# One block of linear attention and a routed expert on one core: q in plain column order, M in seven passes, reciprocals fetched per chunk, weights loaded earlier

## The chip, the core and the metric

The kernel runs on one core of a Trainium2 chip. The core has TensorE (PE, matrix products; PEld is its weight load), VectorE (DVE), ScalarE (ACT), GpSimd (POOL) and SyncE (SP, which here only issues DMAs), and 16 DMA engines that move data between the chip's memory (DRAM) and the on-chip SBUF. TensorE writes to PSUM, eight banks of 2 KB a partition. The metric is the device time of one execution, in microseconds (us).

## The reference

x has 2048 tokens of D = 640 numbers. Two things are added to it.

```python
xn  = layernorm(x)                                  # per token
q, k, v = split(xn @ wqkv)                          # 32 heads of 20 columns
phi(t) = where(t > 0, t + 1, exp(t)) + 1e-6
kv  = einsum("shd,she->hde", phi(k), v)             # 20 x 20 per head
z   = sum over tokens of phi(k)
o   = (phi(q) @ kv) / (phi(q) . z + 1e-6)           # per head
A   = o @ wo

r   = x_B @ w_r                                      # routing score of each token
idx = the 8 tokens with the largest r
y   = (silu(xs @ w_gate) * (xs @ w_up)) @ w_down     # xs: those 8 tokens of xn
B   = xn, with y * sigmoid(r[idx]) added at rows idx

out = x + A + B
```

In the whole program the second part gets xn as its input, so that its residual is xn and the scores are xn @ w_r.

## The kernel before

The tokens are cut into 16 tiles of 128 (T), the 640 columns into 5 chunks of 128 (KC). All of the program is one function. The schedule is manual: each engine executes its instructions in the order in which the code issues them, and semaphores that follow from tiles and buffers let an engine wait for another. So an instruction that waits holds everything behind it on the same engine, and a DMA that waits holds the DMAs behind it on the queue of its issuer. A DMA also waits until an earlier one that used the same one of eight semaphores has landed.

**Start (to L399).** ln_half and ln_aggr take a tile's statistics (VectorE), and a power on GpSimd makes the standard deviation; ln_norm makes xn (L191). TensorE transposes xn of tiles 0 to 2 itself (tr_tile, L200), from tile 3 on a DMA does it (L196). k_mm (L236) and q_mm (L248) are the products with wk and wq. k_mm(0) runs five matmuls of 512 columns and then five of 129 (128 and the column of the scores); behind them come the transposes of tile 1 and their evictions (L206).

**The loop (L401).** Slot t does k_mm(t), ga_mm(t - 1) and q_mm(t) on TensorE; meanwhile VectorE does the statistics of a later tile, the normalisation of a tile with its transpose, and the last steps of phi for q of t - 1 and k of t (L225); ScalarE does the exp and relu halves (L213, L216). Statistics run three tiles ahead and normalisation two. In slot 5 (CATCH) both do one tile more, and from then on are four and three ahead. ga_mm sums xn^T phi(k), from which kv follows as wv^T (xn^T phi(k)). late_loads issues one load a slot on SP: x's last two quarters in slots 2 and 5, w_gate from slot 6, w_up from 9, wv and wo in 12 to 15; w_down follows behind the loop. From slot 12 residual adds xn to x in place (L360) and keep writes the sums to xcp in DRAM (L363); the last four tiles come behind the search for the top eight.

**Behind the loop.** The scores are transposed, the eight largest are found on VectorE, and GpSimd copies their columns of xnT into xsT (L537). Meanwhile TensorE sums the rest of xn^T phi(k): gb1 (L489) columns 384 to 640 of xn, gb2 (L590) the last 128 columns of phi(k). z_mm (L460) sums phi(k) over tokens; zpart goes from rows to partitions by small DMAs (zrel). pden (L571) has the 32 denominators of all tokens: a group of 32 partitions for each block of 512 tokens; ScalarE takes the reciprocal as exp(-ln). Two tiles of gb2 come next, then gate and up (gu, L606), then the rest of gb2.

**q's columns.** q_mm takes every fifth column of wq as one block of weights, `wq[:, kc, m::KC]`, so that partition p of chunk m holds column 5p + m, which belongs to head p // 4 in every chunk. So one tile rb of reciprocals serves all five chunks. It is made by a write of rden to DRAM that repeats each row four times (rscr, L621) and two loads (L625). norm(j) multiplies a block of 512 tokens in place (L632).

**M and the output.** kv is kept block diagonal, masked, in kvT (L670). M (L728) is kv times wo, in q's column order: for each chunk m, 8 blocks of 80 rows of wo make two chained passes of four column groups of 32. M's copies (L737) go to ScalarE for chunks 0, 1 and 3 and VectorE for 2 and 4. y (L688) is made before, copied, and added by GpSimd's indirect DMA to the eight rows of xcp (L697); behind that scatter SP loads xcp back into x_sb (L702). The output of tile t is five chunks of pqT times M (L743); VectorE adds x_sb while reading PSUM (L751), and ACT's and SP's queues write the result in turn (L762). Four PSUM buffers rotate, so tile t + 4 waits for the addition of tile t.

Of the kernel before, what the change touches and what calls it, by code (L numbers as in the profile page):

```python
# [11 lines left out]
H = 32  # L12
# [13 lines left out]
PAD = 16  # L26
# [5 lines left out]
CATCH = 5  # L32
# [12 lines left out]
def kernel(  # L45
# [47 lines left out]
    kvT = sb([EB, PAD + NEB * KC * 2 * PAD], BF16, "kvT")  # L93
# [4 lines left out]
    rscr = dram.tile([NTB * P, TBLK], BF16, name="rscr")  # L98
# [32 lines left out]
    headg = sb([P, NTB, H], BF16, "headg")  # L131
    nc.vector.memset(headg[:], 1.0)
    mask80 = sb([EB, KC, 4, 4], BF16, "mask80")
# [21 lines left out]
    head_select(headg[:], [(0, NTB), (-4, H)], 1, 4)  # L155
# [73 lines left out]
    def k_mm(t, tag="A"):  # L229
# [5 lines left out]
        for kc, (a, b) in order:  # L235
            nc.tensor.matmul(  # L236
                ps[:, a:b],
                lhsT=xnT[:, kc, t * P : (t + 1) * P],
                rhs=wk[:, kc, a:b],
                start=(kc == 0), stop=(kc == KC - 1),  # L240
            )
        return ps

    def q_mm(t, tag="B"):
        ps = pair(tag, f"q{t}")
        for m in range(KC):
            for kc in range(KC):
                nc.tensor.matmul(  # L248
                    ps[:, m * P : (m + 1) * P],
                    lhsT=wq[:, kc, m::KC],  # L250
# [43 lines left out]
    ln_aggr(2)  # L294
# [8 lines left out]
    def small_consts(t):  # L303
# [18 lines left out]
        elif t == 6:  # L322
            head_select(mask80[:], [(0, KC), (-DH, 4), (0, 4)], 1, DH)
# [17 lines left out]
    def late_loads(t):  # L341
        def part(dst, src, a, b):
            nc.sync.dma_start(dst[:, a:b, :], src[:, a:b, :])

        wv_v = wqkv_v[:, :, 2 * D : 3 * D]
        plan = {
            2: (x_sb, x_v, 8, 12), 5: (x_sb, x_v, 12, 16),
            6: (wg, kcF, 0, 2), 7: (wg, kcF, 2, 4), 8: (wg, kcF, 4, 5),
            9: (wu, kcU, 0, 2), 10: (wu, kcU, 2, 4), 11: (wu, kcU, 4, 5),
            12: (wv, wv_v, 0, 2), 13: (wv, wv_v, 2, KC), 14: (wo, wo_v, 0, 4), 15: (wo, wo_v, 4, 8),  # L350
            16: (wd, kcD, 0, 6), 17: (wd, kcD, 6, 12),
        }
        if t in plan:
            part(*plan[t])

# [21 lines left out]
    kp = k_mm(0, "A")  # L377
    tr1a, tr1b = bank("D1", "tr1a").bitcast(BF16), pair("C", "tr1b").bitcast(BF16)
    tr_tile(1, tr1a, 0, 2)
    tr_evict(1, tr1a, 0, 2, nc.scalar.copy)  # L380
    tr_tile(1, tr1b, 2, KC)
    tr_evict(1, tr1b, 2, KC, nc.vector.tensor_copy)
# [18 lines left out]
    for t in range(2, T):  # L401
# [11 lines left out]
        if t > 12:  # L413
            residual(4 * (t - 13) + 3)
        phi_vec(pk[:, t, :], ker, False)
        qer = phi_act(qp, "q")
        if 11 < t < T - 1:
            for u in range(4 * (t - 12), 4 * (t - 12) + 3):
# [3 lines left out]
        if t > 12:  # L422
            keep(4 * (t - 13), 4 * (t - 12))
# [48 lines left out]
    zpart = sb([P, D], F32, "zpart", tag="rb")  # L472
    nc.scalar.copy(zpart[:], zp[:, 0:D])
# [6 lines left out]
    late_loads(T)  # L480
    late_loads(T + 1)
# [54 lines left out]
    for c in range(C):  # L536
# [7 lines left out]
        out=zm[:], in0=headg[:, 0, :].unsqueeze(1).to_broadcast([P, KC, H]),  # L544
# [17 lines left out]
    for t in range(T - 4, T):  # L562
        residual(t)
    keep(T - 4, T)
# [33 lines left out]
    for t in range(2):  # L598
        gb2(t)


    gu = pair("A", "gu")
    for a, w in enumerate((wg, wu)):
# [9 lines left out]
    sg = sb([P, FJ], F32, "sg")  # L613
# [5 lines left out]
    rb = sb([P, S], BF16, "rb")  # L619

    nc.sync.dma_start(  # L621
        rscr[:].rearrange("(p r) n -> p r n", r=4), rden[:].unsqueeze(1).to_broadcast([P, 4, TBLK])
    )
    for j in (0, 2):
        nc.sync.dma_start(  # L625
            rb[:, j * TBLK : (j + 2) * TBLK].rearrange("p (j n) -> p j n", j=2),
            rscr[j * P : (j + 2) * P, :].rearrange("(j p) n -> p j n", j=2),
        )

    def norm(j):  # L630
        sl = pqT[:, :, j * TBLK : (j + 1) * TBLK]
        nc.vector.tensor_tensor(  # L632
            out=sl, in0=sl,
            in1=rb[:, j * TBLK : (j + 1) * TBLK].unsqueeze(1).to_broadcast([P, KC, TBLK]),
            op=ALU.mult,
        )

    for t in range(2, 12):
# [14 lines left out]
    pkv = (bank("D0", "pkv0"), bank("D1", "pkv1"), pair("B", "pkv2"))  # L653
    groups = ((0, 2, 4), (1, 3, 5), (6, 7))

    def kv_mm(i):
        for n, b in enumerate(groups[i]):
# [8 lines left out]

    def kv_evict(i):
        n, w = len(groups[i]), KC * 2 * PAD
        lo, step = groups[i][0], groups[i][1] - groups[i][0]
        nc.vector.tensor_tensor(  # L670
            out=kvT[:, PAD : PAD + NEB * w].rearrange("e (b m c) -> e b m c", b=NEB, m=KC)[
                :, lo : groups[i][-1] + 1 : step, :, 0:PAD
            ],
            in0=pkv[i][0:EB, 0 : n * EB].rearrange("e (b c m) -> e b m c", b=n, m=KC),
            in1=mask80[:].rearrange("e m h j -> e m (h j)").unsqueeze(1).to_broadcast([EB, n, KC, PAD]),
            op=ALU.mult,
        )

    for i in range(3):
        kv_mm(i)  # L680
        kv_evict(i)
    norm(0)
# [39 lines left out]
    for m in range(KC):  # L722
        pm = Acc("CBADC"[m], f"M{m}")
        for a, b in halves:
            for i in range(2):
                for g in range(4):
                    o = PAD + ((2 * g + i) * KC + m) * 2 * PAD - i * PAD
                    nc.tensor.matmul(  # L728
                        pm.at(a, b)[32 * g : 32 * g + 32, :],
# [77 lines left out]
```

## Time and profile before

| What | us |
|---|---|
| three runs | 112.4, 111.48, 112.14 (median 112.14) |
| the profiled execution, whole | 111.62 |
| its span from the first to the last instruction | 109.9 |
| TensorE busy | 105.5 |
| VectorE busy | 86.1 |
| ScalarE busy | 55.1 |
| GpSimd busy | 37.9 |
| moved by DMA | 23.09 MB, mean 210 GB/s |

Stretches in the span: start to 8.84 us, the loop with its first slots to 62.48, the sums and the search to 79.81, kv and y to 82.28, M to 85.00, the output to 107.0, the last writes to 109.9.

In timelines the columns are: start, duration, engine (a q behind it is the engine's sequencer, which issues DMAs), line, operation, output and inputs, count, and in brackets the idle time before it with what ended it. In rows by line: busy time with the mean of one in ns, and idle time before it. In the rows of DMA issues: size of one and the median time from issue to landing.

### The profile page before, as it was taken

The page shows a single profiled execution, that of the slowest core. Times are in us where ns is not written, and L with a number is a line of the kernel's source. Part 1 is how long each engine was busy: PE and PEld are TensorE (multiplying, and loading weights), DVE is VectorE, ACT ScalarE, POOL GpSimd, SP SyncE. Part 2 cuts the span into 40 slices and gives each one's busy share as a digit, 9 for nine tenths or more (in the row PEclk, how much of TensorE's full clock was granted, in tenths as well). Part 3 has the DMA queues.
Part 4 walks back from the last instruction along what each step waited for, and adds up shares of the span by engine and source line. Part 5 has one row for each costly group of instructions (what it writes and reads, how often), then busy time and mean ns, then how long its engine had stood idle before and what let it go on. Part 6 is the DMA issues. An engine that isn't in the chain of part 4 may idle for free.

```text
span 109.9 us, 2999 instructions
## 1 busy us (share of the span) xinstructions
PE 105.5 (96%) x1183; PEld 69.3 (63%) x1183; DVE 86.1 (78%) x205; ACT 55.1 (50%) x102; POOL 37.9 (34%) x83
## 2 busy tenths in 40 slices
PE   6998999999999999999999999999999999999990
PEld 2456866777577766777667744447995555555560
DVE  6889999887999889875999896951348967698680
ACT  4037987778867797777977745068028000000000
POOL 5414195989889955770000000240008100000000
DMA  2998164930569999998859970899541289997333
GB/s 72 335 375 292 33 36 75 283 66 3 118 177 321 220 267 280 316 305 224 290 187 285 292 257 5 232 378 372 175 145 51 15 228 323 340 387 277 128 119 119
DMA packets 25358, 23.09 MB, mean 210 GB/s; under 512 B 10624, under 2 KB 24064, under 8 KB 25344
## 3 DMA queue, kind: packets, MB, share of 16 engines
q1 hardware_dynamic: 22784, 20.43, 66.5%
q10 hardware_dynamic: 2384, 2.43, 6.4%
q8 instruction: 9, 0.15, 0.6%
q0 software_dynamic: 176, 0.04, 0.6%
q14 instruction: 5, 0.04, 0.1%
HBM read 14.94 MB, written 5.81 MB: 189 GB/s over the span
## 4 chain that ended last, share of the span: by engine, by line
PE 76%; DVE 10%; POOL 8%; issue 3%; DVEq 0%; POOLq 0%
PE o L743 14%; PE k L236 13%; PE q L248 13%; PE gbA L489 6%; PE gaC L259 5%; PE warm L271 4%; PE gbC L590 4%; POOL sq L176 3%; DVE st L163 2%; PE gaD L259 2%; DVE pk L225 2%; PE M L728 2%; POOL sc L178 2%; DVE xn L191 2%; PE gu L606 2%
## 5 line engine op out<-in xcount | busy, mean ns | idle before, releaser
L248 PEld LDWEIGHTS <-wq 128*128 128x128 bf16 x400 | 24.2, 117 | 3.4
L236 PE MATMUL k<-wk,xnT 128*128 128x512 bf16 (+1 forms) x160 | 24.8, 301 | 0.3 <-ACT xnT L206 0.3
L248 PE MATMUL q<-xnT,wq 128*128 128x128 bf16 x400 | 24.9, 220 | 0.0
L743 PEld LDWEIGHTS <-pqT 128*128 128x128 bf16 x165 | 12.8, 98 | 9.3
L236 PEld LDWEIGHTS <-xnT 128*128 128x128 bf16 x160 | 12.3, 98 | 8.5 <-ACT xnT L206 0.9
L213 ACT ACTIVATE eq<-q 128x640 bf16<-128x640 f32 x16 | 11.2, 703 | 10.5 <-PE q L248 10.5
L225 DVE SCALAR_TENSOR_TENSOR pk<-ek,rk 128x640 bf16<-128x640 bf16 x16 | 13.2, 824 | 3.6 <-ACT rk L216 3.4
L743 PE MATMUL o<-M,pqT 128*128 128x512 bf16 x110 | 15.8, 300 | 0.0
L176 POOL TENSOR_TENSOR sq<-sq,half 128x1 bf16<-128x1 bf16 x16 | 12.5, 778 | 6.2 <-DVE sc L175 4.0
L163 DVE BATCH_NORM_STATS2 st<-x_sb 128x6 f32<-128x320 bf16 x32 | 14.1, 480 | 0.4 <-DMA x_sb<-in_A_x_dram 0.4
L225 DVE SCALAR_TENSOR_TENSOR pqT<-eq,rq 128x640 bf16<-128x640 bf16 x16 | 13.2, 823 | 0.7 <-ACT rq L216 0.7
L213 ACT ACTIVATE ek<-k 128x640 bf16<-128x640 f32 x16 | 11.3, 705 | 1.6 <-PE k L236 0.4
L751 DVE TENSOR_TENSOR o_t<-o,x_sb 128x640 bf16<-128x640 f32 x11 | 8.8, 820 | 3.3 <-DMA x_sb<-xcp 1.7
L216 ACT ACTIVATE rq<-q 128x640 bf16<-128x640 f32 x16 | 11.2, 700 | 0.0
L216 ACT ACTIVATE rk<-k 128x640 bf16<-128x640 f32 x16 | 11.2, 699 | 0.0
L259 PE MATMUL gaC<-pk,xn 128*128 128x512 bf16 x32 | 9.5, 378 | 0.2 <-DVE pk L225 0.2
L537 POOL COPY xsT<-xnT 128x5 bf16 x8 | 1.9, 312 | 21.7 <-DVE icol L551 21.7
L178 POOL TENSOR_TENSOR sc<-sq,neg 128x1 f32<-128x1 bf16 x12 | 8.6, 716 | 0.9
L191 DVE TENSOR_SCALAR xn<-x_sb,sc 128x640 bf16<-128x640 bf16 (+2 forms) x17 | 6.9, 412 | 1.2 <-POOL sc L179 1.0
L489 PE MATMUL gbA<-pk,xn 128*128 128x512 bf16 x32 | 7.3, 380 | 0.0
L360 DVE TENSOR_TENSOR x_sb<-x_sb,xn 128x640 bf16<-128x640 bf16 x16 | 7.0, 482 | 0.0
L259 PEld LDWEIGHTS <-xn 128*128 128x128 bf16 x48 | 4.0, 97 | 4.1 <-issue 0.4
(152 smaller groups left out, 120.4 us busy)
## 6 DMA issues: line engine op xcount, KB each, us to landing
xcp<-x_sb SPq DMA_DIRECT2D x4, 640.0 KB, 5.2
x_sb<-in_A_x_dram SPq DMA_DIRECT2D x3, 640.0 KB, 4.7
wd<-in_B_w_down_dram SPq DMA_DIRECT2D x2, 960.0 KB, 6.6
x_sb<-xcp SPq DMA_DIRECT2D x3, 640.0 KB, 6.8
wg<-in_B_w_gate_dram SPq DMA_DIRECT2D x2, 768.0 KB, 6.6
wu<-in_B_w_up_dram SPq DMA_DIRECT2D x2, 768.0 KB, 5.3
out_dram<-o_t ACTq DMA_DIRECT2D x8, 160.0 KB, 2.7
out_dram<-o_t SPq DMA_DIRECT2D x7, 160.0 KB, 3.4
```

Source lines behind the costliest of these rows:

```text
L163: nc.vector.bn_stats(out=stat[t][:, h, :], in_=x_sb[:, t, h * HW : (h + 1) * HW])
L176: nc.gpsimd.tensor_tensor(out=sq[:, 1:2], in0=sq[:, 0:1], in1=half[:], op=ALU.pow)
L178: nc.gpsimd.tensor_tensor(out=sc[:, 1:2], in0=sq[:, 1:2], in1=neg1[:], op=ALU.pow)
L191: nc.vector.tensor_scalar(out=xn[:, t, a:b], in0=x_sb[:, t, a:b], scalar1=sc[:, 0:1], scalar2=sc[:, 1:2], op0=ALU.subtract, op1=ALU.mult,)
L213: nc.scalar.activation(e[:], ps[:, 0:D], AF.Exp)
L216: nc.scalar.activation(r[:], ps[:, 0:D], AF.Relu)
L225: nc.vector.scalar_tensor_tensor(out=dst, in0=ea, scalar=1.0, in1=ra, op0=ALU.min, op1=ALU.add)
L236: nc.tensor.matmul(ps[:, a:b], lhsT=xnT[:, kc, t * P : (t + 1) * P], rhs=wk[:, kc, a:b], start=(kc == 0), stop=(kc == KC - 1),)
L248: nc.tensor.matmul(ps[:, m * P : (m + 1) * P], lhsT=wq[:, kc, m::KC], rhs=xnT[:, kc, t * P : (t + 1) * P], start=(kc == 0 and m in (0, 4)) ...
L259: nc.tensor.matmul(gaC[:, c * TBLK : (c + 1) * TBLK] if c < 2 else gaD[:], lhsT=xn[:, t, c * P : (c + 1) * P], rhs=pk[:, t, 0:TBLK], start ...
L489: nc.tensor.matmul(gbA[:, (c - 3) * TBLK : (c - 2) * TBLK], lhsT=xn[:, t, c * P : (c + 1) * P], rhs=pk[:, t, 0:TBLK], start=(t == 0), stop ...
L743: nc.tensor.matmul(ps, lhsT=pqT[:, m, t * P : (t + 1) * P], rhs=M[:, m, a:b], start=(m == 0), stop=(m == KC - 1),)
```

## The change

- q_mm takes plain columns, `m * P : (m + 1) * P`. Column m * 128 + p belongs to head (128 m + p) // 20, so the reciprocals differ by chunk. rden is written to rscr with each row five times, in four pieces, and 20 loads (one per block of 512 tokens and chunk, two of them on ACT's queue) bring rows repeated four times into rb of 5 x 2048, which takes the place of xnT. norm takes 2, 2, 4, 4 and 4 tiles.
- kvT has 96 columns a block; kv is evicted in two pieces. M has main passes for each chunk, and the row groups that straddle two blocks get a second pass, which two chunks share: 3 + 3 + 1. The order of chunks in the output is 0, 1, 3, 4, 2.
- The first four output tiles are copied by ScalarE without x; VectorE adds x to them in SBUF later.
- The transposes of tile 1 go between the halves of k_mm(0), and tile 2's aggregate behind them.
- The extra tile's statistics are split over slots 5 and 6 and its normalisation goes to slot 7.
- w_gate starts in slot 3, w_up in 7, w_down in 10, wv in 6, 9 and 10. Tiles 0 to 2 of the sums of x go into slots 9 to 11, and all are written to xcp inside the loop.
- gate and up follow the denominators at once.

```diff
-    for t in range(2):
-        gb2(t)
     gu = pair("A", "gu")
...
+        for n, (kc, (a, b)) in enumerate(order):      # k_mm
+            if n == KC and between is not None:
+                between()
...
-                    lhsT=wq[:, kc, m::KC],
+                    lhsT=wq[:, kc, m * P : (m + 1) * P],
...
-            6: (wg, kcF, 0, 2), 7: (wg, kcF, 2, 4), 8: (wg, kcF, 4, 5),
-            9: (wu, kcU, 0, 2), 10: (wu, kcU, 2, 4), 11: (wu, kcU, 4, 5),
-            12: (wv, wv_v, 0, 2), 13: (wv, wv_v, 2, KC), 14: (wo, wo_v, 0, 4), 15: (wo, wo_v, 4, 8),
-            16: (wd, kcD, 0, 6), 17: (wd, kcD, 6, 12),
+            2: (x_sb, x_v, 8, 12), 3: (wg, kcF, 0, 2), 4: (wg, kcF, 2, 4), 5: (x_sb, x_v, 12, 16),
+            6: (wg, kcF, 4, 5), 7: (wu, kcU, 0, 2), 8: (wu, kcU, 2, 4), 9: (wu, kcU, 4, 5),
+            10: (wd, kcD, 0, 5), 11: (wd, kcD, 5, 10), 12: (wd, kcD, 10, FC),
+            13: (wo, wo_v, 0, 4), 14: (wo, wo_v, 4, 8),
...
-        for u in (t + 3, t + 4) if t == CATCH else (t + 3 + (t > CATCH),):
-            if u < T:
-                ln_stats(u)
-        for u in (t + 2, t + 3) if t == CATCH else (t + 2 + (t > CATCH),):
+        if t == 6:
+            ln_half(9, 1)
+            ln_aggr(9)
+        u = t + 3 + (t > 5)
+        if u < T:
+            ln_stats(u)
+        if t == 5:
+            ln_half(9, 0)
+        for u in (t + 2, t + 3) if t == 7 else (t + 2 + (t > 7),):
...
-    nc.sync.dma_start(
-        rscr[:].rearrange("(p r) n -> p r n", r=4), rden[:].unsqueeze(1).to_broadcast([P, 4, TBLK])
-    )
-    for j in (0, 2):
-        nc.sync.dma_start(...)                        # rb, 2 blocks each
+    for a, b in ((0, H), (H, 2 * H), (2 * H, 3 * H), (3 * H, P)):
+        nc.sync.dma_start(rscr_v[a:b], rden_v[a:b])   # REP = 5
+    def rb_load(j):
+        src = rscr[j * H * REP : (j + 1) * H * REP, :].rearrange("(m s) n -> s m n", m=KC)
+        for m in range(KC):
+            (nc.scalar if (j, m % 2) == (0, 1) else nc.sync).dma_start(
+                rb[:, m, j * TBLK : (j + 1) * TBLK],
+                src[:, m, :].unsqueeze(1).to_broadcast([P // 4, 4, TBLK]),
+            )
+    for j in range(NTB):
+        rb_load(j)
...
-    for m in range(KC):                               # M: two chained passes a chunk
-        pm = Acc("CBADC"[m], f"M{m}")
+    for (ca, ta), (cb, tb) in (((0, "B"), (1, "C")), ((3, "A"), (4, "D"))):
+        pa, pb = Acc(ta, f"M{ca}"), Acc(tb, f"M{cb}")
+        main_a, rest_a = m_rows(ca, pa)
+        main_b, rest_b = m_rows(cb, pb)
+        run(main_a)
+        run(main_b)
+        run(rest_a + rest_b)
+        m_copy(ca, pa, nc.scalar.copy)
+        m_copy(cb, pb, nc.vector.tensor_copy)
+    pm = Acc("B", "M2")
+    run(m_rows(2, pm)[0])
+    m_copy(2, pm, nc.scalar.copy, nc.vector.tensor_copy)
+    norm(2, 4)
+    norm(4, 8)
...
+    for t in range(NPRE):                             # NPRE = 4
+        po = o_mm(t)
+        o_pre[t] = o_tile(t)
+        for a, b in po.spans:
+            nc.scalar.copy(o_pre[t][:, a:b], po.at(a, b))
+    for t in range(NPRE):
+        nc.vector.tensor_tensor(out=o_pre[t][:], in0=o_pre[t][:], in1=x_sb[:, t, :], op=ALU.add)
+        (nc.scalar, nc.sync)[t % 2].dma_start(out_v[:, t, :], o_pre[t][:])
+    norm(8, 12)
```

More of the change, by code (lines that the diff above doesn't have):

```diff
@@ L31 @@
 LAST = (0, 320, 512, 640)
-CATCH = 5
 BF16 = mybir.dt.bfloat16
@@ L417 @@
         if 11 < t < T - 1:
-            for u in range(4 * (t - 12), 4 * (t - 12) + 3):
+            for u in range(4 * (t - 12) + 4, 4 * (t - 12) + 7):
                 residual(u)
@@ L650 @@
     nc.scalar.copy(GT[:, :, TBLK:D], gbC[:, 0:D].rearrange("p (c f) -> p c f", c=KC))
[L653 to L657, printed above, removed]
+    pkv = bank("D0", "pkv0"), bank("D1", "pkv1")
+    for i in range(2):
+        for n in range(4):
+            b = 4 * i + n
             for kc in range(KC):
```

175 lines of the change are left out of this document (93 added, 82 removed).

## The prediction

> **What bounds the kernel now.** I read the page's head first, then busy time by stretch, then TensorE's waits. The head:
>
> ```profile
> span 109.9 us, 2999 instructions
> ...
> PE 105.5 (96%) x1183; PEld 69.3 (63%) x1183; DVE 86.1 (78%) x205; ACT 55.1 (50%) x102; POOL 37.9 (34%) x83
> ```
>
> TensorE is busy 96% of the span. A mean hides stages, so the next view cuts the span (columns: stretch, length, busy time of each engine, granted clock, DMA share, GB/s):
>
> ```profile
> 8.84:29.44 20.60, 20.37 (x231) 14.95 (x232) 18.48 (x45) 16.55 (x32) 14.62 (x34) 1.00 0.47 103
> 29.44:62.48 33.04, 33.04 (x372) 24.17 (x372) 29.25 (x60) 25.04 (x48) 15.20 (x30) 1.00 1.02 260
> ...
> 82.28:85.00 2.72, 2.72 (x82) 1.58 (x74) 2.32 (x2) 2.18 (x5) 2.08 (x1) 1.00 0.21 70
> 85.00:107.00 22.00, 22.00 (x165) 12.70 (x165) 17.39 (x25) 0.15 (x1) 0.54 (x1) 1.00 0.71 227
> ```
>
> From 8.84 us to 107.0 us TensorE lacks only 0.23 us, at a clock of 1.00. So an edit pays if it takes matmul time or one of TensorE's few waits away, and costs if it makes TensorE wait. Its waits by releaser leave two of note behind the warm-up; both stand in brackets in the rows of terms 1 and 2, and the change touches both, and M.
>
> **Term 1, the start.** The transposes of tile 1 follow all ten matmuls of k0, and k1 waits for their eviction:
>
> ```profile
> 8.84 1.56 PE L236 MATMUL k<-wk,xnT 128*128 128x512 bf16 x10 [0.30 <-ACT xnT L206]
> ...
> 8.68 0.71 ACT L213 ACTIVATE ek<-k 128x640 bf16<-128x640 f32 x1
> ...
> 9.86 0.18 ACT L373 CAST r_all<-k 128x1 bf16<-128x1 f32 x1
> 10.23 0.27 PE L248 MATMUL q<-xnT,wq 128*128 128x128 bf16 x2
> ```
>
> Afterwards they stand between the five wide and the five narrow matmuls of k0, so the evictions run beside the narrow ones. The wait, at most 0.3 plus the pipeline's restart, some 0.4 in all, shrinks. But q0 writes the bank that k0 held, and may not start before r_all is copied, 10.04 now. That copy ends ScalarE's work on k0, which begins at 8.68, behind the eviction, and then near 8.5, when the narrow matmuls end. So q0 moves from 10.23 to about 10.0: I take 0.25, bounds 0 and 0.4. The statistics of tile 2 finish behind tile 1's eviction, which moves tile 2's normalisation by some 0.2; its transposes are needed only after q0.
>
> **Term 2, slot 5 of the loop.** A plain slot and the long one by stretch, the rows that end it, and the statistics by line:
>
> ```profile
> 24.23:27.66 3.43, 3.43 (x42) 2.49 (x41) 2.78 (x9) 2.65 (x5) 3.12 (x10) 1.00 0.10 22
> 27.66:31.64 3.98, 3.75 (x42) 2.62 (x41) 3.95 (x9) 2.65 (x5) 3.21 (x9) 1.00 0.55 91
> ...
> 27.47 0.45 DVE L191 TENSOR_SCALAR xn<-x_sb,sc 128x640 bf16<-128x640 bf16 x1 [0.58 <-POOL sc L179]
> 28.57 0.82 DVE L225 SCALAR_TENSOR_TENSOR pk<-ek,rk 128x640 bf16<-128x640 bf16 x1
> 29.44 0.59 PE L259 MATMUL gaC<-pk,xn 128*128 128x512 bf16 x2 [0.23 <-DVE pk L225]
> ...
> L163 DVE BATCH_NORM_STATS2 st<-x_sb 128x6 f32<-128x320 bf16 x32 | 14.1, 480 | 0.4 <-DMA x_sb<-in_A_x_dram 0.4
> ...
> L167 DVE BATCH_NORM_AGGREGATE mv<-st 128x2 bf16<-128x12 f32 x16 | 3.3, 208 | 0.5
> ```
>
> A slot takes 3.43, this one 3.98: VectorE takes statistics and normalisation of an extra tile in slot 5, stands 0.58 for GpSimd, and hands pk over late. The edit spreads this: half the statistics in slot 5, the rest in 6, the extra normalisation in 7. Without the second half (0.48), the aggregate (0.21), the wait (0.58) and the normalisation (0.45), pk ends not at 29.39 but near 27.7, well before TensorE first asks at 29.21. Slot 6 takes on 0.48 + 0.21, slot 7 the 0.45; VectorE's work in a plain slot, 2.78, leaves 0.65, so it stays abreast. So the 0.55 go; I take 0.5, bounds 0 and 0.55.
>
> **Term 3, M.** Its stretch and the output's stand above (from 82.28 and from 85.00); the copies by line:
>
> ```profile
> L737 DVE CAST M<-M 128x640 bf16<-128x640 f32 x2 | 1.6, 824 | 0.3 <-PE M L728 0.3
> ...
> L737 ACT CAST M<-M 128x640 bf16<-128x640 f32 x2 | 1.3, 695 | 0.3 <-PE M L728 0.3
> ```
>
> M is 5 chunks x 2 passes over 640 columns: 2.72 / 10 = 0.272 a pass, four column groups side by side. Seven passes are 1.90: 0.82 less. (The two passes of the leftovers fill two groups of four and cost the same.) Less cover is the price: the copies now end last. ScalarE copies M0, M3 and the wide part of M2 in line, about 0.7, 0.7, 0.6, from 0.82 + 0.2 after the stage's start: ready at 1.7, 2.4 and 3.0. M2's matmuls also wait for M0's copy, as they share a bank: 0.1. An output tile takes 22.00 / 16 = 1.375, a chunk of it 0.275; tile 0 takes M2 last, from 2.0 + 4 x 0.275 = 3.1, with VectorE's narrow copy perhaps behind ScalarE's: up to 0.3 late. I take 0.82 - 0.27 = 0.55, bounds 0.2 and 0.8.
>
> **Edits at nothing.** Weight loads and matmuls, then the rows that the other edits lean on:
>
> ```profile
> L248 PEld LDWEIGHTS <-wq 128*128 128x128 bf16 x400 | 24.2, 117 | 3.4
> ...
> L590 PEld LDWEIGHTS <-xn 128*128 128x128 bf16 x80 | 4.5, 98 | 0.7 <-issue 0.7
> ...
> 30.25 1.40 PE q L248 x25
> ...
> 75.62 2.90 PE gbC L590 x50
> ...
> 70.66 1.94 POOL L537 COPY xsT<-xnT 128x5 bf16 x8 [21.66 <-DVE icol L551]
> 71.96 1.26 PE L571 MATMUL pden<-pqT,zm 128*32 128x512 bf16 x20
> ...
> 69.96 0.18 DVE L539 TENSOR_REDUCE zc<-zrel 128x5 f32<-128x20 f32 x1
> ...
> L360 DVE TENSOR_TENSOR x_sb<-x_sb,xn 128x640 bf16<-128x640 bf16 x16 | 7.0, 482 | 0.0
> ```
>
> q in plain columns: the strided weight load is 19 ns longer than a plain one, but the matmuls follow each other every 1.40 / 25 = 56 ns, and behind plain loads every 2.90 / 50 = 58. Loads do not set the pace: 0. The other bound is the output's pace, 640 columns in 0.275, which is 55 ns per 128: 16 x 25 x 1 ns = 0.4. The Trainium skill (SBUF — State Buffer, section Door 1: The DMA port swizzle) holds that an access falling on a new 16-byte line each time pays a penalty; the 117 against 98 agrees, and by it q would gain; that is a rival below.
>
> Gate and up next to the denominators: the same matmuls in another order; their inputs xsT are copied by 72.6, the denominators end at 73.2, both shift alike. The four sums of x that move into slots 9 to 12 are 0.48 each and fill the 0.65 that VectorE has over; without it each would cost up to 0.48. w_down's parts and the last 640 KB of x now stand in SP's queue ahead of the column sums' loads. Those are reduced at 69.96, 0.5 of work follows, and the denominators start at 71.96: 1.5 of delay are free, more would reach TensorE one for one. Two wider evictions instead of three for kvT hide beside y's matmuls.
>
> **Term 4, the reciprocals' transfers.** The issues in order, DMA by stretch (last column GB/s), landings, the issue of x's tiles 4 to 7 with its landing, the ACT queue's writes over the span and in 87.5 to 96, and VectorE's first multiplication:
>
> ```profile
> 74.65 0.59 SPq L621 DMA_DIRECT2D rscr<-rden  x1
> 79.89 0.98 SPq L625 DMA_DIRECT2D rb<-rscr  x2
> 87.19 2.90 SPq L702 DMA_DIRECT2D x_sb<-xcp  x6
> ...
> 80.90:83.20 2.30, 2.30 (x93) 1.81 (x94) 1.48 (x3) 0.61 (x2) 0.28 (x1) 1.00 0.72 228
> ...
> rscr<-rden SPq DMA_DIRECT2D x1, 512.0 KB, 5.1
> rb<-rscr SPq DMA_DIRECT2D x2, 256.0 KB, 2.5
> ...
> L702 SPq DMA_DIRECT2D x_sb<-xcp x1: 467/467/467, 88.5 to 88.5; - x1
> ...
> DMA to landing us min/median/max: 5.7/5.7/5.7
> ...
> out_dram<-o_t ACTq DMA_DIRECT2D x8, 160.0 KB, 2.7
> ...
> out_dram<-o_t ACTq DMA_DIRECT2D x3, 160.0 KB, 6.0
> ...
> 82.43 1.49 DVE L632 TENSOR_TENSOR pqT<-pqT,rb 128x2560 bf16<-128x2560 bf16 x1 [0.73 <-DMA rb<-rscr]
> ```
>
> Now 512 KB are written and read. Afterwards 640 KB are written in four pieces, and 20 loads of 128 KB, 2.6 MB, are read, 18 from SP. All of it starts 0.75 (terms 1 and 2) earlier: 73.9. The old write stood behind w_down and x in its queue; alone it lands like the other short transfers, 2.5. First loads 76.4; the first block needs three from SP and two from ACT, the third of SP's at 77.4, landed 79.9. VectorE, free at 81.70 now and then at 80.95, finds it there with 1.0 to spare; each microsecond beyond holds VectorE, and so M's copies and the output, by one.
>
> What is late next is x's return: on SP it queues behind these loads. 18 issues x 0.48 end at 85.0, landed by 87.5: hardly a delay, as the return waits for the scatter, 87.19 - 0.75 = 86.4. At the 228 GB/s of the two old loads, 2.6 MB need 11.5, from 77.5 to 89: 2.6 late. Tiles 4 to 7 landed at 88.5 + 5.7 = 94.2, 7.0 behind the scatter; afterwards at 93.4 to 96.0. Tiles 0 to 3 are taken out by ScalarE without x, so x is first needed when tile 8 wants tile 4's bank: at 83.7 (85.0 - 0.75 - 0.55) + 8 x 1.375 = 94.7, less an addition of 0.82: 93.85. So TensorE stands 0 to 2.1. I take 0.1: of the two rates I hold the issue's for the nearer, as 0.59, 0.49 and 0.48 each are SP's own rows and the 228 spans just two loads, with the start and end of both.
>
> The Trainium skill (DMA: Bandwidth & Descriptors, section Bandwidth) speaks against cutting: batch to 1 MB, at 64 KB it measured 138 GB/s. By that, as an estimate, the loads would need more than the 11.5.
>
> **Sum.** 0.25 + 0.5 + 0.55 - 0.1 = 1.2 off. Against the profiled execution (span 109.9 and 1.72 around it, 111.62) that is 110.4; it lies 0.52 below the median of the three runs, so on 112.14 the forecast is 110.9.
>
> **Rivals.**
>
> The scatter and the return of x are held up (slower). For it: writes that landed in 2.7 took 6.0 beside the return of x. If the loads hold the scatter by as much, 3.3, it lands at 89.7, tiles 4 to 7 at 96.7, and TensorE stands 2.85: 112.14 - 1.3 + 2.85 = 113.7. It decides from a landing of 95.15, where the gain is eaten. Against it: loads are issue-paced. The Trainium skill (same page, section Queues, rings and completion order) says the DMA engines alternate between queues packet by packet; by that the scatter isn't starved; no run here shows the two side by side. Chance 0.20.
>
> Transposes late in the loop (slower). Landings of the loop's transposes, and the queue under weights:
>
> ```profile
> DMA to landing us min/median/max: 2.6/3.9/5.7
> ...
> 30.70:55.00 24.30, 24.30 (x275) 17.73 (x274) 20.80 (x44) 18.57 (x35) 14.50 (x26) 1.00 1.09 271
> ```
>
> Weights now start in slot 3, while the transposes have a lead of two slots until slot 7. Tile 8's is issued near 30.0 (slot 6's start on VectorE, 27.7, with the 0.69 added there, a tile's statistics, 1.17, and the normalisation, 0.45); its matmul opens slot 8, at 31.64 + 3.43 - 0.75 = 34.3: 4.3, where 5.7 has been seen. Both tiles 8 and 9 at 5.7 cost 2 x 1.4: 110.9 + 2.8 = 113.7. Against: the DMA share of 0.10 in slot 4 leaves nearly a whole slot free for what starts earlier. Chance 0.12.
>
> Seven passes that don't shorten anything, as the copies gate the output: 110.9 + 0.55 = 111.5. Chance 0.10.
>
> q gains too: 110.9 - 0.4 = 110.5. Chance 0.08.
>
> **How the numbers follow.** The forecast has 0.50, its own range 110.4 to 111.9 (terms at their best and at their least). Within 1% (111.0 to 113.3, about what a measurement can tell from no change): 0.16 of the forecast's, 0.08 of the seven passes', 0.03 from each slower rival: 0.30. Faster: 0.34 + 0.02 + 0.08 = 0.44. Slower: 0.17 + 0.09 = 0.26. The range runs from all terms at their best (110.0) over the slower rivals, 113.9.
>
> **What would show it.** k1 near 8.45; slot 5 at 3.43; M in 1.9; tile 0 of the output under 0.4 late; SP's last rb issue before 85.5; no wait of TensorE for VectorE at tile 8. I am wrong if TensorE waits there for an addition that waits for x, or at k8 or k9 for a transpose.

## The result, and the profile after

The changed kernel takes 117.55 us (median of six runs, 116.17 to 120.04) against 111.65 for the kernel before (median of six). It is slower by a ratio of 1.047, 95% interval 1.041 to 1.052, and outside the range of the forecast. The profiled execution is the longest of the six, 120.04; it and the other long one, 119.27, are left out of the ratio, which compares the other four (median 116.91) with the kernel before. These four have no profile; two versions below that issue as many loads wait 3.7 and 4.0 where this execution waits 5.2. The page's head, and busy time by stretch (columns as before):

```profile
span 118.3 us, 2975 instructions
...
PE 106.6 (90%) x1151; PEld 69.2 (59%) x1151; DVE 84.7 (72%) x206; ACT 58.5 (49%) x106; POOL 36.5 (31%) x83
...
PEclk9999999999999999999999999999999999558998
```
```profile
8.64:28.21 19.57, 19.05 (x221) 14.05 (x221) 18.14 (x45) 15.70 (x30) 13.61 (x32) 1.00 0.75 182
28.21:62.58 34.37, 34.37 (x380) 24.67 (x381) 31.30 (x67) 26.04 (x50) 16.79 (x32) 1.00 1.15 277
82.28:85.38 3.10, 1.79 (x48) 1.02 (x41) 1.61 (x3) 2.07 (x4) 1.75 (x1) 1.00 0.43 114
85.38:96.41 11.03, 11.03 (x80) 6.08 (x79) 4.14 (x7) 2.93 (x6) 0.00 (x0) 1.00 0.73 214
96.41:101.61 5.20, 0.00 (x1) 0.10 (x2) 3.17 (x5) 0.00 (x0) 0.00 (x0) 0.88 1.01 323
99.50:100.50 1.00, 0.00 (x0) 0.00 (x0) 0.00 (x0) 0.00 (x0) 0.00 (x0) 0.91 1.04 339
101.61:106.61 5.00, 5.00 (x19) 2.43 (x19) 4.33 (x6) 0.00 (x0) 0.00 (x0) 0.50 0.75 274
106.90:107.30 0.40, 0.40 (x5) 0.20 (x4) 0.16 (x1) 0.00 (x0) 0.00 (x0) 0.69 0.93 346
```

Up to the loop's end nothing is gained or lost: the matmuls behind it (pr) start at 62.58, before at 62.41. The output starts at 85.38 against 84.93 (0.45 late). At 96.41 TensorE stops for 5.20. Its granted clock falls within that wait, between 99.5 and 100.5, and is back at 1.00 at some 107.1, so about 5.5 us of matmuls run at half speed: from tile 8 to the end TensorE needs 118.3 - 101.61 = 16.7, where eight tiles of 1.375 and the last writes of 2.9 make 13.9, so 2.8 more. 0.45 + 5.2 + 2.8 = 8.45; the spans differ by 8.4. TensorE's waits, and the end of the chain that ended last (start, us):

```profile
PE o L776 <- DVE o_t L784: 5.2, 1, 5.2
PE o L776 <- DVE M L755: 1.1, 1, 1.1
...
PE k L239 <- DMA xnT<-xn: 0.5, 1, 0.5
```
```profile
91.06 0.60 SPq L640
91.77 0.54 SPq L706
92.83 0.43 SPq L706
93.31 7.33 DMA x_sb<-xcp
100.73 0.83 DVE o_t L784
101.61 5.49 PE o L776 x20
```

The chain tells the cause: SP issues loads of reciprocals (L640) one after another until 91.06 + 0.60, only then x's return (L706); tiles 4 to 7 land at 93.31 + 7.33 = 100.64, and tile 8 waits for tile 4's addition. In order of time:

```profile
74.82 2.62 SPq L635 DMA_DIRECT2D rscr<-rden  x4
77.62 14.04 SPq L640 DMA_DIRECT2D rb<-rscr  x18
83.77 0.82 DVE L650 TENSOR_TENSOR pqT<-pqT,rb 128x1280 bf16<-128x1280 bf16 x1 [1.96 <-DMA rb<-rscr]
85.38 2.88 PE L776 MATMUL o<-M,pqT 128*128 128x512 bf16 x20 [1.10 <-DVE M L755]
91.77 3.10 SPq L706 DMA_DIRECT2D x_sb<-xcp  x6
94.46 0.49 DVE L803 TENSOR_TENSOR o_t<-o_t,x_sb 128x640 bf16<-128x640 bf16 x1 [5.30 <-DMA x_sb<-xcp]
```
The loads by tile (min, median and max of an issue in ns), and the scatter among the DMA issues, before and after (last column: us to landing):

```profile
L640 SPq DMA_DIRECT2D rb<-rscr x18: 513/602/1282, 77.6 to 91.1; - x18
```
```profile
xcp<-y_sb,rowu POOLq DMA_INDIRECT x1, 4.3
...
xcp<-y_sb,rowu POOLq DMA_INDIRECT x1, 4.5
```

An issue takes 602 ns (median), not 480. With the gaps between them, of which 0.9 is a wait until an earlier load lands, 18 loads take 14.04, 0.78 each. The first block lands 3.8 later than forecast (83.7 for 79.9), so VectorE waits 1.96 with M's copies behind it, and TensorE 1.10. The scatter lands in 4.5 (4.3 before). Weight loads of q fell from 117 to 98 ns, yet 25 matmuls of q still take 1.40.

### The profile page after: what moved, and what is told of

It reads as the page before. It is cut to its first block, busy times and chain, and to the rows that moved or that the text cites. A ratio compares the mean times of both kernels' runs of the same rounds, so it can differ in the third digit from the quotient of the medians.

```text
span 118.3 us, 2975 instructions
## 1 busy us (share of the span) xinstructions
PE 106.6 (90%) x1151; PEld 69.2 (59%) x1151; DVE 84.7 (72%) x206; ACT 58.5 (49%) x106; POOL 36.5 (31%) x83
## 4 chain that ended last, share of the span: by engine, by line
PE 59%; DMA 19%; SPq 8%; DVE 5%; issue 3%; ACT 2%; ACTq 0%; DVEq 0%
PE k L239 17%; PE q L251 15%; PE o L776 8%; SPq L640 7%; DMA x_sb<-xcp 6%; PE gbA L507 6%; DMA xnT<-xn 5%; PE gaC L262 5%; DMA rb<-rscr 4%; DMA x_sb<-in_A_x_dram 3%; PE gaD L262 2%; DVE o_t L784 2%; DVE st L164 1%; DMA rscr<-rden 1%; SPq L706 1%
## 5 line engine op out<-in xcount | busy, mean ns | idle before, releaser
L251 PEld LDWEIGHTS <-wq 128*128 128x128 bf16 x400 | 23.7, 98 | 3.7
L776 PE MATMUL o<-M,pqT 128*128 128x512 bf16 x110 | 18.4, 330 | 6.3 <-DVE o_t L784 5.2
L776 PEld LDWEIGHTS <-pqT 128*128 128x128 bf16 x165 | 13.9, 104 | 17.4 <-issue 5.8
L179 POOL TENSOR_TENSOR sc<-sq,neg 128x1 f32<-128x1 bf16 x12 | 9.5, 793 | 0.9
L784 DVE TENSOR_TENSOR o_t<-o,x_sb 128x640 bf16<-128x640 f32 x8 | 6.5, 820 | 4.3 <-PE o L776 2.8
L650 DVE TENSOR_TENSOR pqT<-pqT,rb 128x2560 bf16<-128x2560 bf16 (+1 forms) x5 | 6.1, 1218 | 2.6 <-DMA rb<-rscr 2.6
L555 POOL COPY xsT<-xnT 128x5 bf16 x8 | 1.1, 207 | 21.1 <-DVE icol L569 21.1
```

Source lines behind the costliest of these rows:

```text
L179: nc.gpsimd.tensor_tensor(out=sc[:, 1:2], in0=sq[:, 1:2], in1=neg1[:], op=ALU.pow)
L251: nc.tensor.matmul(ps[:, m * P : (m + 1) * P], lhsT=wq[:, kc, m * P : (m + 1) * P], rhs=xnT[:, kc, t * P : (t + 1) * P], start=(kc == 0 an ...
L776: nc.tensor.matmul(ps, lhsT=pqT[:, m, t * P : (t + 1) * P], rhs=M[:, m, a:b], start=(m == M_ORDER[0]), stop=(m == M_ORDER[-1]),)
L784: nc.vector.tensor_tensor(out=o_t[:, a:b], in0=ps, in1=x_sb[:, t, a:b], op=ALU.add)
```

## The experiments

Each changes the changed kernel, but for three that change the kernel before. Medians are followed by the ratio to the kernel before, run beside it (111.57 to 111.85), and its interval. Waits, starts and clocks are those of the one profiled execution.

**Is it SP's order, or the load on the DMA engines?** Three edits. Ten loads instead of twenty, the same bytes:

```diff
-    for j in range(NTB): rb_load(j)                # 5 loads of 512 columns each
+    for a, b in ((0, 1), (1, NTB)):                # 5 of 512, 5 of 1536 columns
+        for m in range(KC): rb_load(m, a, b)
```


> The same 2.6 MB of reciprocals arrive in ten loads instead of twenty (five of 128 KB for the first block of tokens, five of 384 KB for the other three), eight of them from SP instead of eighteen. Theory S (x's return stands behind the loads in SP's in-order queue, and the queue is paced by the issue, 0.6 us a load whatever its size): SP is through with them by 82.5, the first x_sb<-xcp is issued when the scatter lands, at 87.2 to 87.5 instead of 91.8; tiles 4 to 7 of x land at 94.5 to 96.5; TensorE waits at tile 8 for 0 to 1 instead of 5.2, the clock stays at 1.00, and the time is 111.5 to 113. Theory D (the DMA engines are full with 2.6 MB of reciprocals, and x's return comes late whichever way it is issued): tiles 4 to 7 land at 99 or later, TensorE still waits over 3, the time is 115 or more. Third possibility: the issue is paced by bytes, then a load of 384 KB takes 1.8 to issue and x's return starts at 90 to 91.8.

x's return from another queue:

```diff
-        nc.sync.dma_start(x_sb[:, a:b, :], xcp_v[:, a:b, :])
+        nc.gpsimd.dma_start(x_sb[:, a:b, :], xcp_v[:, a:b, :])
```


> The six loads that bring x back are issued by GpSimd's queue instead of SP's; the twenty loads of reciprocals stay. Theory S: the first x_sb<-xcp is issued as the scatter lands, at 87.2 to 87.5, while SP is still issuing reciprocals until 91; tiles 4 to 7 land at 96 to 98, TensorE waits at tile 8 for 0.5 to 2.5 instead of 5.2, the time is 112 to 114. Theory D: x's loads share the DMA engines with the reciprocals, tiles 4 to 7 land at 99 or later, the wait stays over 3.5, the time is 115.5 or more.

Twenty loads of 128 columns instead of 512:

> Left out: three quarters of the reciprocals; every load fetches 128 of its 512 columns, and the other tiles of a block are multiplied by those of its first tile. Twenty loads with as many rows as before, a quarter of the bytes. Theory S: an issue on SP still takes 0.6, x's return is issued at 91 to 92 and tiles 4 to 7 land at 98 to 99.5; TensorE waits 2.5 to 4.5 at tile 8; the time is 114.5 to 116.5. Theory D: what slows the issue is the load on the DMA engines, so with a quarter of the bytes an issue takes 0.4 or less, x's return starts as the scatter lands, at 87.2 to 87.5, and the time is 111 to 112.

Measured: 113.92 (1.022, 1.017 to 1.027), 114.46 (1.025, 1.018 to 1.032), 117.47 (116.19 to 119.65). The loads by tile, of the third and of the first:

```profile
L640 SPq DMA_DIRECT2D rb<-rscr x18: 513/602/1312, 77.1 to 89.9; - x18
```
```profile
L638 SPq DMA_DIRECT2D rb<-rscr_w x8: 513/576/1389, 78.0 to 84.7; - x8
```

The timelines, of the third, the second and the first:

```profile
90.65 3.09 SPq L711 DMA_DIRECT2D x_sb<-xcp  x6
98.53 0.69 PE L781 MATMUL o<-M,pqT 128*128 128x512 bf16 x2 [3.72 <-DVE o_t L789]
```
```profile
87.11 4.21 POOL L706 DMA_DIRECT2D x_sb<-xcp  x6 [2.97 <-DMA xcp<-y_sb,rowu]
97.57 2.88 PE L776 MATMUL o<-M,pqT 128*128 128x512 bf16 x20 [1.84 <-DVE o_t L784]
```
```profile
86.44 2.88 PE L775 MATMUL o<-M,pqT 128*128 128x512 bf16 x20 [1.80 <-DVE M L754]
89.14 2.90 SPq L705 DMA_DIRECT2D x_sb<-xcp  x6
```

And the scatter in the chain of the first:

```profile
83.23 5.90 DMA xcp<-y_sb,rowu
```

With a quarter of the bytes an issue still takes 602 ns, the 18 take 13.4 for 14.04, and x's return is issued nearly as late (90.65); in the run with ten loads, five of its eight on SP with three times the bytes, the median is 576. All these loads have 128 rows, so a price per row would look the same; but x's own loads, of up to 512 rows, take 0.43 to 0.54 an issue in the changed kernel. So the price is per load, and theory S holds for the 5 us. With fewer loads or another queue the wait at tile 8 is 0 or 1.84, and the clock stays at 1.00. (Of the run with ten loads three more executions have a mean clock of 0.985; they have no profile that would show where it fell.) The three times all lie above those that theory S expected (111.5 to 113, 112 to 114, 114.5 to 116.5), so something else is left. With ten loads the scatter took 5.90 beside the wide ones (x's return starts at 89.14, not 87.3), and the first block came later still, 1.80 at tile 0. With the other queue tiles 0 and 12 waited 0.91 and 0.57.

**The clock.** Thirty matmuls that nobody reads fill the wait:

```diff
+            if t == 7:
+                for _ in range(30):
+                    nc.tensor.matmul(po.banks[0][:, D : 2 * TBLK], ...)   # 128x384
```


> Thirty matmuls that nobody reads (128x384, some 4.8 us in all) stand between tile 7 of the output and tile 8, in columns of tile 7's PSUM pair that hold nothing; the waits for x stay. Theory C (the half clock after tile 8's start is the price of TensorE's 5 us of idleness, and some 2.5 of the loss): x's tiles land as late as in the changed kernel, tile 8 starts at 100.5 to 102, but the granted clock stays at 1.00 and tiles 8 to 11 take 1.4 each; the time is 114 to 115.5. If the clock falls for another reason, it falls here too: 117 to 118.5.

Measured: 116.76 (1.043, 1.038 to 1.048). By stretch, the filling matmuls and the tiles behind them:

```profile
97.50:102.60 5.10, 5.10 (x33) 2.99 (x31) 3.10 (x5) 0.00 (x0) 0.00 (x0) 1.00 1.00 312
102.60:107.00 4.40, 4.39 (x33) 2.43 (x32) 4.40 (x8) 0.00 (x0) 0.00 (x0) 1.00 0.92 332
```

Tile 8 starts at 102.67, as late after pr as in the changed kernel (38.4 and 39.0), but the clock stays at 1.00 and the rest takes 116.6 - 102.67 = 13.9 instead of 16.7. So the half clock follows from the idleness. The medians differ by 0.8 only, less than expected (114 to 115.5), and the interval overlaps that of the changed kernel, 1.041 to 1.052. The profiled execution started late (pr at 64.25), and the changed kernel's other runs lost less clock than its profiled one (mean over the span 0.971 to 0.985 against 0.967). How much of the median is the clock stays open.

**Where x is needed.** Eight tiles taken out of PSUM without x, NPRE = 8 and the last two multiplications ahead of the additions:

> Eight output tiles instead of four are taken out of PSUM by ScalarE without x, and the last two multiplications by reciprocals stand ahead of the additions; x comes back as late as in the changed kernel. If the late x costs time only where TensorE needs a bank that an addition holds, then tile 8 starts at 96.4 to 97 with no wait, the next such bank is tile 8's own, wanted by tile 12 at 102, its addition waits for x until 102.5 to 103.5, TensorE waits 1 to 2 there, the clock stays at 1.00, and the time is 112.5 to 114.5. If VectorE's additions, all of them later, end last instead: 115 or more.

Measured: 114.14 (1.027, 1.021 to 1.033). As expected, tile 8 doesn't wait, tile 12 waits 1.46, and the clock is 1.00. But it isn't x that ends the wait of tile 12. Tile 8's addition stands until an output has landed whose buffer it reuses, while its x had landed at 99.7 (timeline):

```profile
101.52 0.82 DVE L784 TENSOR_TENSOR o_t<-o,x_sb 128x640 bf16<-128x640 f32 x1 [1.72 <-DMA out_dram<-o_t]
```

Then both remedies, then tile 0's multiplication cut off, then the weights' requests as in the kernel before:

> Both remedies for the late x: its return is issued by GpSimd's queue, and eight tiles are taken out of PSUM without it. If the late x is all that the change lost behind tile 0, TensorE waits nowhere from tile 1 to tile 15 for more than 0.3, tile 0 starts at 84.5 to 85.4 (as in the other kernels with these loads), the last tile ends 22 to 22.3 later, the clock stays at 1.00, and the time is 110.8 to 112, the kernel before or up to 0.7 below it. If additions or the reuse of the output's buffers end last in its place, it is 112.5 or more.

> As the run with both remedies, and the first multiplication by reciprocals is cut: tile 0 alone ahead of M's copies on VectorE, tile 1 behind them. If M's copies gate tile 0 of the output (0.9 to 1.1 of waiting for VectorE's copy of M), tile 0 starts 0.3 to 0.45 earlier than with both remedies alone, at 84.1 to 84.3, and the time falls as much: 110.4 to 111.6. If not, no difference.

> As the run with the cut multiplication, and the loop's weights are requested in the very slots and pieces of the kernel before, w_down after the loop. If the early and larger weight requests make the transposes late, TensorE waits for no transpose in the loop (in four of the profiles with the change's requests, and with other early pieces, 0.2 to 1.6 were lost there) and pr starts at 61.8 to 62.1; the price is w_down's 1.9 MB in the queue ahead of the reciprocals' write, whose landing moves by 0 to 1.5. The time is 110.2 to 111.5 if the price is small, 111.5 to 113 if the first block lands 1.5 later.

Measured: 119.66 (1.067), 118.28 (1.058), 119.26 (1.063), all far off. The timeline of the first of them:

```profile
78.08 14.38 SPq L640 DMA_DIRECT2D rb<-rscr  x18
88.11 4.20 POOL L706 DMA_DIRECT2D x_sb<-xcp  x6 [3.05 <-DMA xcp<-y_sb,rowu]
102.14 1.49 DVE L650 TENSOR_TENSOR pqT<-pqT,rb 128x2560 bf16<-128x2560 bf16 x1 [7.90 <-DMA rb<-rscr]
107.63 4.73 PE L776 MATMUL o<-M,pqT 128*128 128x512 bf16 x20 [5.54 <-DVE o_t L784]
```

SP has issued the last block by 92.5, yet it lands at 102.1. x, issued from 88.11 on by the other queue, is under way beside it, and a load of reciprocals now takes up to 10.6 to land, against 5.2 in the changed kernel. VectorE, on which I had put this multiplication ahead of the additions, stood before it for 7.90. So theory D is right where SP's order no longer decides: some 5.2 MB of reciprocals and x must pass in the order of their use. In the cut version tile 0 starts at 84.10 with 0.4 of waiting instead of 0.9; with the old weights' requests no transpose is late and pr starts at 61.94. Those two local expectations held.

**The first block, and the weights.** The first block written alone and loaded at once, the others written by GpSimd's queue; weights from slot 6 on, in larger pieces; and these with eight tiles without x:

> The first block's reciprocals are written by SP alone and loaded at once (three loads from SP, two from ACT); GpSimd's queue writes the other three blocks beside it, and SP loads them with five wide loads. Theory F (the first block lands late, at 83 to 84.8, because its loads stand in the queue behind the other writes and beside the later loads; VectorE waits for it with M's copies behind it): the block lands at 80 to 81.5, VectorE does not wait for it, tile 0 of the output starts at 84.0 to 84.4 instead of 85.4 (changed kernel) and 86.4 (ten loads); SP issues x's return as the scatter lands, 87 to 88.5; TensorE waits 0 to 1.5 at tile 8; the time is 111 to 112.5. Rival: the writes by GpSimd take the DMA engines at the same time and the first block lands at 82.5 or later; then tile 0 starts at 85 or later and the time is 113 or more.

> The weights of the loop are requested as late as in the kernel before (w_gate from slot 6 on, nothing in slots 3 and 4); all else as in the changed kernel. If the early weights make the transposes late (k6 waited 0.52 for its one), k6 and the later matmuls of the loop wait for no transpose, the column-sum matmuls pr behind the loop start at 61.9 to 62.2 instead of 62.65, 0.3 to 0.6 before those of the kernel before (62.48). If not, k6 waits as before and pr stays at 62.4 to 62.8. What lies behind the loop is untouched: TensorE still waits some 5 at tile 8, the time is 116 to 118, and the difference of half a microsecond can't be read from the time, only from the trace.

> The early first block, the old times of the weights and eight tiles without x together. If the three effects add up: pr at 61.9 to 62.2, tile 0 of the output at 83.6 to 84.1, no wait of TensorE at tile 8 and under 0.5 at tile 12, clock 1.00; the time is 110.3 to 111.2, that is 0.5 to 1.4 below the kernel before, which is what the terms 1 to 3 of the forecast promised. If the gains of terms 1 to 3 are not there, it stays at 111.5 or more.

Measured: 115.63 (1.040), 119.44 (1.066), 115.76 (1.036). In the first the block still lands at 82.5, the rival's figure, though tile 0 starts at 84.16; then tile 4 waits 2.18 for the second block. The scatter took 7.8, beside wide loads once more. In the second k6 waits for no transpose, but by the timeline k9 does:

```profile
39.05 1.56 PE L239 MATMUL k<-wk,xnT 128*128 128x512 bf16 x10 [1.11 <-DMA xnT<-xn]
```

In the third it is 1.62, and tiles 0, 4 and 12 of the output wait 0.59, 1.14 and 1.04: the three effects do not add up. Larger pieces in slots 7 and 9 moved the lateness instead of removing it.

**Terms 1 and 2 alone**, on the kernel before: both, term 1, term 2.

> The kernel before with nothing but the terms 1 and 2 of the forecast: the transposes of tile 1 between the wide and the narrow matmuls of k0, and the statistics of the extra tile spread over slots 5 to 7. The forecast's sum for the two is 0.75 (bounds 0 and 0.95): pr at 61.7, 110.9 against 111.65. From the traces with the whole change, in which q0 stands at 10.19 as before and pr at 61.9 to 62.2 where no transpose was late, I now expect 0.3 to 0.55 from term 2 alone and nothing from term 1: pr at 61.9 to 62.2, the time 0.3 to 0.6 below the kernel before, 111.1 to 111.3. If the transposes come late here as well, although the weights are requested as before, the lead that the extra tile gave was what kept them early, and the gain is 0 or less.

> The kernel before with term 1 alone, the transposes of tile 1 inside k0. The forecast took 0.25 (0 to 0.4). From the traces I expect nothing: k1 starts 0.2 earlier, q0 at 10.2 as before, the time within 0.3 of the kernel before, 111.4 to 111.9.

> The kernel before with term 2 alone, the extra tile's statistics spread over slots 5 to 7, weights requested as before. The forecast took 0.5 (0 to 0.55). If the gain is real and not taken back: slot 5 at 3.43, pr at 61.9 to 62.1, the time 111.0 to 111.3. If the lead of the transposes is what it costs: waits of 0.3 or more for xnT near k7 to k10, and the time 111.4 to 112.

Measured: 111.86 (1.001, 0.998 to 1.004), 111.59 (0.999, 0.996 to 1.002), 111.97 (1.002, 1.000 to 1.004). None of them shows a gain. The intervals of the first and the last exclude the 0.75 and the 0.5 that were forecast; that of term 1 alone would still hold its 0.25. The last of the three shows why term 2 gives nothing; it waits nowhere for pk, but its timeline has, at k9:

```profile
38.23 1.56 PE L236 MATMUL k<-wk,xnT 128*128 128x512 bf16 x10 [0.34 <-DMA xnT<-xn]
```

k6 to k7 is 30.88 - 27.45 = 3.43 there (3.82 before), k8 to k9 38.23 - 34.30 = 3.93 (3.43 before). What slot 5 of VectorE no longer costs, tile 9 loses to its transpose. With term 1 alone q0's third matmul waits 0.24 for wq, with both terms 0.36.

**The transfers made small.** The quarter of the bytes and the ten loads together (three quarters of the reciprocals are left out):

> Left out: three quarters of the reciprocals, as in the run with a quarter of the bytes; and now in ten loads, eight of them on SP. The transfers then cost about what those of the kernel before did. If the transfers are the whole loss, x's return starts as the scatter lands, tile 0 of the output starts 21.7 to 21.9 behind pr (83.78 - 62.05 = 21.73 in the run with twenty small loads, 22.52 in the kernel before), TensorE waits nowhere in the output, and the time is 110.2 to 111.2, below the kernel before. If it is 111.5 or more, M's seven passes or plain columns cost something else.

Measured: 110.75 (0.993, 0.990 to 0.996). The output (rows of the chain) runs without a gap, and x comes as the scatter lands (timeline):

```profile
83.75 2.82 PE o L780 x20
87.93 4.08 PE o L780 x30
93.37 4.08 PE o L780 x30
```
```profile
81.75 0.82 DVE L650 TENSOR_TENSOR pqT<-pqT,rb 128x1280 bf16<-128x1280 bf16 x1 [0.46 <-DMA rb<-rscr_w]
86.37 3.54 SPq L710 DMA_DIRECT2D x_sb<-xcp  x6
```

Tile 0 starts at 83.68, 21.63 behind pr (62.05); before it was 22.52, so 0.89 is gained. Of this 0.67 lies in M's stage: from M's first matmul to the output's first it is 83.68 - 81.53 = 2.15, before 84.93 - 82.11 = 2.82. The other 0.22 lies ahead of it, between the denominators and the products with wv. There the change moves only gate and up on TensorE, and TensorE takes 7.46 for the stretch (79.59 - 72.13 in the changed kernel; its other versions within 0.01 of that) where the kernel before takes 79.64 - 71.96 = 7.68. What the transfers cost is the difference to this run, 117.55 - 110.75 = 6.8 between the medians, 6.0 by the two ratios.

**All bytes, in the order of use.** The last block's loads behind x's tiles 0 to 7:

```diff
     for a, b in ((0, 1), (1, 2), (2, 4), (4, 8), (8, 12), (12, 16)):
         nc.sync.dma_start(x_sb[:, a:b, :], xcp_v[:, a:b, :])
+        if b == 8:
+            rb_load(NTB - 1)
```


> All bytes, all on SP, only the order is another: the last block's five loads are issued behind x's tiles 0 to 7, the last multiplication stands behind tile 8's addition on VectorE, eight tiles are taken out without x, tile 0's multiplication is cut off. With both remedies and GpSimd's queue the last block landed at 102 and VectorE stood before it, with 5.5 of waiting at tile 12. Theory S with the bytes in mind (what must come first has to be issued first): x's return starts as the scatter lands, 86.9 to 87.5, tiles 4 to 7 land at 94 to 96, the last block at 96 to 99, tiles 8 to 11 of x at 97 to 100; TensorE waits at tile 12 for 0 to 0.5; the time is 110.8 to 112.2. Theory D (too many bytes in any order): TensorE waits over 2 somewhere from tile 4 on, the time is 113 or more.

Measured: 117.77 (1.048). The order did its work (x's return at 88.02), but tile 8's addition waited for something else, the landing of tile 0's output, whose buffer it reuses (timeline):

```profile
103.93 0.82 DVE L787 TENSOR_TENSOR o_t<-o,x_sb 128x640 bf16<-128x640 f32 x1 [6.77 <-DMA out_dram<-o_t]
```

So the same with memory of their own for tiles 8 to 11 and NPRE = 6, and then with M1's copy ahead of tile 0's multiplication:

> All bytes; the last block's loads behind x's tiles 0 to 7; six tiles taken out without x; tile 0's multiplication alone ahead of M's copies; tiles 8 to 11 of the output in memory of their own. If issuing in the order of need is enough: x's tiles 4 to 7 land at 94.5 to 96, tiles 8 to 11 by 100, the last block by 99; TensorE waits 0.4 to 0.6 at tile 0 and under 0.5 in all behind it; the clock stays at 1.00; the time is 110.8 to 112.0. If 5.2 MB of reciprocals and x are too many in any order, TensorE waits 1.5 or more at tile 12 or before, and the time is 112.5 or more.

> The same, and VectorE copies M1 before it multiplies tile 0. If VectorE's order sets tile 0's start, it starts 0.2 to 0.35 earlier than without, and the time falls by as much. If the first block's landing at 82.7 to 83.5 sets it, it starts no earlier than 83.8 to 84.1 and the time is the same within 0.2.

Measured: 112.87 (1.007, 1.004 to 1.011) and 112.59 (1.006, 1.003 to 1.010). The timeline of the first:

```profile
87.75 1.99 SPq L706 DMA_DIRECT2D x_sb<-xcp  x4
100.22 0.82 DVE L787 TENSOR_TENSOR ox<-o,x_sb 128x640 bf16<-128x640 f32 x1 [2.36 <-DMA x_sb<-xcp]
102.50 2.89 PE L779 MATMUL o<-M,pqT 128*128 128x512 bf16 x20 [1.18 <-DVE pqT L650]
```

Some 4.7 of the 5.9 between the medians are won back. 1.18 is left at tile 12, since tiles 8 to 11 of x land at 100.2; before their load SP had waited 2.1 until a load of reciprocals had landed. M1's copy first lets tile 0 start at 84.05 for 84.54 with no wait; the medians differ by less than their intervals. No version with all the bytes beats the kernel before.

## Why the prediction was wrong

- **The step that failed is term 4**, "So TensorE stands 0 to 2.1. I take 0.1: of the two rates I hold the issue's for the nearer, as 0.59, 0.49 and 0.48 each are SP's own rows". TensorE stood 5.20, at tile 8 and for an addition that waited for x, as the prediction's last sentence had named it. The choice between the rates was right, the figure was not: these loads took 0.602 each, 0.78 with the waits between, began at 77.62, not 76.4 (the write itself began at 74.82, not 73.9, as terms 1 and 2 had moved nothing), and the last issue ended at 91.7, not 85.0. x's return went out 4.6 later than before, 91.77 for 87.19, and its four tiles landed in 7.3 instead of 5.7. The upper bound was wrong too: I had worked out its late end by bytes (2.6 late) and not by a dearer issue, though 0.59 was quoted; 76.4 + 18 x 0.59 gives 87.0, already behind the scatter's 86.4. And the forecast's "own range 110.4 to 111.9 (terms at their best and at their least)" left this bound out: with 2.1 its upper end is 112.14 - 0.2 + 2.1 = 114.0. (In term 4 itself 94.7 less 0.82 is 93.88, not 93.85.)
- **A size left out of the sum**: TensorE's idleness itself costs. The clock was 0.50 for about 5.5 us of matmuls behind the wait, which cost 2.8 in the profiled run. The Trainium skill (TensorE: Matmul & The Clock Gate, section Part 1: The HAM clock gate) says that an idle window of some 3.4 us halves the clock until a busy one has passed. The traces agree: behind 5.20 of idleness, 4.01 (weights from slot 6 on) and 3.72 (a quarter of the bytes) the clock read 0.50, behind 2.18 and 1.84 it read 1.00.
- **The first rival** foresaw the loss's place, x's return, but not its mechanism. In the changed kernel the scatter was not held up (4.5 against 4.3). By the Trainium skill (DMA: Bandwidth & Descriptors, section Queues, rings and completion order) the DMA engines alternate between queues by packets; the 4.5 agrees. Beside the wide loads, with rows of 3 KB, the scatter did take 5.9 to 7.8, so there the rival's mechanism is seen. In the changed kernel it was SP's own queue that held x. Its price, 2.85, and the chance, 0.20, were both too small.
- **The first block**: "landed 79.9. VectorE ... finds it there with 1.0 to spare" failed by 3.8. The writes cost SP 2.62 and the last landed in 2.9, the loads of the first block in up to 5.2, where 2.5 was taken for each. "Each microsecond beyond holds VectorE, and so M's copies and the output, by one" was right in kind and too dear: VectorE stood 1.96 and TensorE 1.10, and with a quarter of the bytes VectorE stood 0.89 and TensorE not at all.
- **Term 3**: forecast 0.55, of 0.82; measured 0.67 where the block is there in time, within the bounds. Of the copies' price of 0.27 some 0.15 was paid; M2's wait on M0's copy was 0.2. In the changed kernel the gain is hidden behind the late block. Gate and up behind the denominators, put at nothing, gave 0.22.
- **Term 2** fell: 0.39 of 0.5 is gained from k6 to k7 and given back to a late transpose, at k9 with term 2 alone and at k6 in the changed kernel (0.52). That is the second rival, whose price of 1.4 a tile was too high and whose tiles, 8 and 9, were off in part. **Term 1** shows in the trace, but no gain of time is measured: in the changed kernel k1 starts 0.20 and q0 0.16 earlier (8.64 and 10.07), and where term 1 is tested without the rest, q0 then waits for wq, which the forecast hadn't counted. In the six profiles of the changed loop in which TensorE waits for no transpose, pr starts at 61.9 to 62.2, 0.2 to 0.5 ahead of the kernel before: part of the 0.75 is there when the transposes are in time.
- **q in plain columns** costs and gives nothing, as forecast (25 matmuls 1.40 before and after); the fourth rival fell with it.

## What to carry to other kernels

Count DMA issues on a queue as serial work with a price per load, measured on loads of the same pattern, and look at what stands last in that queue; the bytes are a second limit behind it. A remedy that lets x pass by another queue only pays if what it overtakes isn't needed sooner. A gain on an engine that then waits for a transfer is no gain until the transfer comes in time: measure the compute with the transfers made small before paying for the transfers.

## What the runs showed of the hardware

- An issue on SP of a load that repeats each row four times takes 0.60 us whether it carries 32 or 128 KB (median 0.58 where five of eight carry 384 KB); the two plain loads of the kernel before took 0.36 and 0.57.
- In a wait of 5.20 us without matmuls TensorE's granted clock fell to 0.50, some 3.1 to 4.1 us after the last matmul, and about 5.5 us of matmuls ran at it; waits of 3.72 and 4.01 halved it too. Behind waits of 2.18, 1.84 and 1.80 it read 1.00.
- With x on a second queue, loads that SP had issued by 92.5 landed as late as 102.1.
- The indirect scatter landed in 4.2 to 4.8 us in the profiles with loads of 128 KB, in 5.9, 7.3 and 7.8 in those with loads of 384 KB (4.3 in the kernel before).
- Executions of the same loop differ by tenths, as its transposes land sooner or later: of thirteen profiles with the change's weight requests five waited for one or two, 0.2 to 0.9 in all, two for 0.1, and six didn't.
